# Fixing TensorE's instruction order in a decode-attention plus MLP kernel: mask products, PV rounds and output products at new places

## The chip, the cores and the metric

The kernel runs on one core of one Trainium2 chip. The metric is the device time of one execution in microseconds (us). The time before is the median of 8 executions. Engines are named as the profile names them: PE is TensorE (PEld its weight loads), DVE is VectorE, ACT is ScalarE, POOL is GpSimd, SP is SyncE, whose queue issues nearly all of the DMAs.

## The reference

Two blocks share one input of two rows and are added to it. Block A is one decode step of attention over the last 2048 positions of a cache, and block B is a squared-ReLU MLP.

```python
B, Sq, D = 2, 1, 576;  Hq, Hkv, Sk, Dh = 32, 16, 8192, 128;  F = 4608
W = min(4096, max(256, Sk // 4))                       # 2048
xn = (x - mean(x)) / sqrt(var(x) + 1e-5)
# A: attention of one query position, two query heads to a KV head
q = (xn @ wq).reshape(B, Sq, Hq, Dh).transpose(0, 2, 1, 3)
k = repeat(k_cache[:, :, Sk - W:, :], 2, axis=1);  v = repeat(v_cache[:, :, Sk - W:, :], 2, axis=1)
p = softmax(einsum("bhqd,bhkd->bhqk", q, k) * Dh ** -0.5)
attn = einsum("bhqk,bhkd->bhqd", p, v).transpose(0, 2, 1, 3).reshape(B, Sq, Hq * Dh) @ wo
# B: MLP
h = relu(einsum("bsd,df->bsf", xn, w1) + b1) ** 2
return x + attn + einsum("bsf,fd->bsd", h, w2) + b2
```

All tensors are bf16. Together 53.6 MB are read from HBM: 16.8 MB of K, as much of V, and the four weights.

## The kernel before, in words

**Units.** Attention is cut into 8 units, each of 4 KV heads of one batch row (`u` in the code; `NU` is 8). A unit's K is one DMA of 2 MB, its V another. Both go into a pool of six buffers (`kvpool`), which later also takes three of the five pieces of `w2`. A load waits until the unit that had its buffer has read it for the last time: K in its transposes, V in its PV products.

**One step.** `step(u)` does these things for a unit:

- `transposes(u, g)`, g from 0 to 7: four products with an identity (line 288) turn K tiles of f32 pairs into the PSUM tile `kT_ps`, of which there are three. Even groups are copied out by ACT (line 293), odd ones by DVE (line 295).
- `scores(u, 0)` after group 5 and `scores(u, 1)` after group 7: eight products each (line 307) into `sc_ps`, of which there are two. The first product of a unit is the head mask product (line 301): it writes a large negative number wherever a query row and a key belong to different heads.
- `softmax(u)`: a row maximum on DVE (`mx`, line 316), a maximum over partitions on POOL (`gmax`), the bias `nb` on DVE, the exponential on ACT (`pr`, line 327) and a transpose on DVE (`pT`, line 329).
- For unit u-2: `pv_sum` (line 339: the sums of the softmax, put together by one small f32 product), four rounds of `pv` (line 352: four products each), the mixing of the four PV parts by four chained DVE operations into `acc` (lines 361 and 364), and `pv_out` (line 376: the "o product", one small f32 product that puts `acc` into the layout for `wo`).

**Ends.** Units 0 to 3 and 4 to 7 are gathered in two halves. After a half is complete, DVE forms `ws` (lines 381, 385), and `wo_acc` multiplies it with half of `wo` (32 products, line 239) into `out_ps`. The MLP's first product (`mlp_h_block`, line 406), its squared ReLU and nine transposes (line 420) stand between unit 6 and unit 7. Its second product (`mlp_o`, line 239) comes after everything of the attention, and its last piece (`mlp_tail`, line 442) closes the kernel. It is followed by one addition on DVE and two small stores.

**Order.** A scheduler orders the instructions of each engine by what is ready; the DMAs on SP stay in the order in which they are traced. An instruction given to `tc.keep_in_program_order` keeps the traced order among those so marked on its engine. In the kernel before, only the products of `scores` and `pv` and the four that put x and b2 into `out_ps` are marked. So the scheduler placed the rest of PE's work: the head mask product of a unit stands one step ahead, in front of the transposes of the step before its own, and at the end of a step the o product of unit u-2 and the sum product of unit u-1 stand in front of that mask product. The order of PE at a step's end before is therefore: four PV rounds, `scores(u, 1)`, o product of u-2, sum product of u-1, mask product of u+2, transposes of u+1.

Of the kernel before, what the change touches and what calls it, by code (L numbers as in the profile page):

```python
# [16 lines left out]
def kernel(  # L17
# [68 lines left out]
    keep = ctx.enter_context(tc.tile_pool(name="keep", bufs=3))  # L86
    psum = ctx.enter_context(tc.tile_pool(name="psum", bufs=1, space=bass.MemoryType.PSUM))

    x2d = A_x.rearrange("b s d -> (b s) d")
# [110 lines left out]
    for c in range(NFULL):  # L200
        nc.tensor.transpose(out=pro_ps[:, c, :], in_=xn_sb[:, c:NFULL * P:NFULL], identity=ident[:B, :B])  # L201
    for sg in range(S):
        nc.tensor.transpose(out=pro_ps[:, NFULL + sg, :], in_=xr_sb[:, sg, :], identity=ident[:B, :B])
    xnT = const.tile([P, NXN, B], BF16, name="xnT")
# [31 lines left out]

    def out_acc(lhsT, rhs_of, start=False, stop=False, pin=False):
        for i in range(2):
            mm = nc.tensor.matmul(out_ps[32 * i:32 * i + B, :], lhsT=lhsT, rhs=rhs_of(i * OH, (i + 1) * OH),  # L239
                                  start=start, stop=stop, skip_group_check=True)  # L240
            if pin:
                tc.keep_in_program_order(mm)

# [6 lines left out]
    def q_block(c):  # L250
        for k in range(2):
            for g in range(NG4):
                rhs, xc = w_rows(wq_tiles, c, g * QW + k * QB, QB, LQ)
                nc.tensor.matmul(q_ps[k][32 * g:32 * g + B, :], lhsT=xnT[:, xc, :], rhs=rhs,  # L254
                                 start=(c == 0), stop=(c == KC - 1), skip_group_check=True,
                                 tile_position=(0, 32 * g))
        if c == KC - 1:
            qrow = const.tile([RB, QW], BF16, tag="row", name="qrow")
            nc.vector.tensor_copy(out=qrow[:, 0:QB], in_=q_ps[0][0:RB, :])
            nc.scalar.copy(out=qrow[:, QB:QW], in_=q_ps[1][0:RB, :])  # L260
            qT_ps = psum.tile([P, QH, P], BF16, tag="misc", name="qT_ps")
            for i in range(QH):
                nc.tensor.transpose(out=qT_ps[:, i, 0:RB], in_=qrow[:, i * Dh:(i + 1) * Dh],
                                    identity=ident[0:RB, 0:RB])
            qT_v = qT_ps[:].rearrange("p i (g s) -> p i g s", s=32)
            for b in range(B):
                nc.vector.tensor_copy(out=qT_all[:, b, :].rearrange("p (g i) -> p i g", g=NG4), in_=qT_v[:, :, :, b])
            qe_ps = psum.tile([P, 2 * NU, NC], F32, tag="sm", name="qe_ps")
            for e in range(2):
                nc.tensor.matmul(qe_ps[:, e * NU:(e + 1) * NU, :], lhsT=par[:, e, :, :].rearrange("p a i -> p (a i)"),  # L270
                                 rhs=qT_all[:].rearrange("p b h -> p (b h)"), start=True, stop=True)
# [7 lines left out]
    def transposes(u, g):  # L279
# [6 lines left out]
        for i in range(PG):  # L286
            q = g * PG + i
            nc.tensor.transpose(out=kT_ps[:, i, :], in_=k_sb[:, 2 * q * Dh:2 * (q + 1) * Dh].bitcast(F32),  # L288
                                identity=ident_f[:])
# [7 lines left out]
    def scores(u, w):  # L297
        tq, b = divmod(u, B)
        if w == 0:
            sc_tiles[u] = psum.tile([P, NT, 32], F32, tag="sc", bufs=2, name=f"sc_ps_{u}")  # L300
            nc.tensor.matmul(sc_tiles[u][:].rearrange("p t s -> p (t s)"), lhsT=qhead[:], rhs=khead[:],  # L301
                             start=True, stop=False, skip_group_check=True)
        sc_ps = sc_tiles[u]
        kT = kT_tiles.pop((u, w))[:].rearrange("p t s e -> p e t s")
        for e in range(2):
            for k in range(4):
                mm = nc.tensor.matmul(sc_ps[32 * k:32 * (k + 1), :, :],  # L307
                                      lhsT=qz[:, e, b * NQ + tq, w, :, :].rearrange("p j c -> p (j c)"),
                                      rhs=kT[:, e, :, 32 * k:32 * (k + 1)], start=False, stop=(w == 1 and e == 1),
                                      skip_group_check=True, tile_position=(0, 32 * k))  # L310
                tc.keep_in_program_order(mm)

# [21 lines left out]
    def pv_sum(u):  # L334
        tq, b = divmod(u, B)
        if u % (2 * B) == 0:
            sm_tiles[tq // 2] = psum.tile([P, B * Dh + 2 * B], F32, tag="sm", name=f"sm_{tq // 2}")
        rs = sm_tiles[tq // 2][:, B * Dh + u % (2 * B):B * Dh + u % (2 * B) + 1]
        nc.tensor.matmul(rs, lhsT=samec[:].rearrange("p x c -> p (x c)"), rhs=sum_tiles.pop(u)[:],
                         start=True, stop=True, skip_group_check=True)  # L340
# [6 lines left out]
    def pv(u, i):  # L347
        pv_ps, f = pv_cur[u]
        v = v_tiles[u][:].rearrange("p (w t x) -> p t w x", w=2, t=NT)
        for k in range(4):  # L350
            t = 4 * i + k
            mm = nc.tensor.matmul(pv_ps[32 * k:32 * (k + 1), :, :].rearrange("m (w a) d -> m w (a d)", w=2),  # L352
                                  lhsT=pT_tiles[u][:, t, :], rhs=v[:, t, :, :], start=(i == 0),
                                  stop=(i == NT // 4 - 1), skip_group_check=True, tile_position=(0, 32 * k))
            tc.keep_in_program_order(mm)
        if i == NT // 4 - 1:
            acc = None
            for j in range(4):
                nx = work.tile([P, Dh], F32, tag=f"acc{j % 2}", name=f"acc_{u}_{j}")
                if j == 0:  # L360
                    nc.vector.tensor_scalar(out=nx[:], in0=pv_ps[:, j, :], scalar1=f[:, j:j + 1], scalar2=None,  # L361
                                            op0=ALU.mult)
                else:
                    nc.vector.scalar_tensor_tensor(out=nx[:], in0=pv_ps[:, j, :], scalar=f[:, j:j + 1], in1=acc[:],  # L364
                                                   op0=ALU.mult, op1=ALU.add)
                acc = nx
            pv_cur[u] = acc
            pT_tiles.pop(u)

    wo_state = {}  # L370

    def pv_out(u):
        tq, b = divmod(u, B)
        t, half = divmod(tq, 2)
        sm = sm_tiles[t]
        nc.tensor.matmul(sm[half * (P // 2):(half + 1) * (P // 2), b * Dh:(b + 1) * Dh],  # L376
                         lhsT=tohead[:].rearrange("p c x -> p (c x)"), rhs=pv_cur.pop(u)[:], start=True, stop=True,
# [18 lines left out]
    def mlp_h_start():  # L396
        mlp["ps"] = [psum.tile([P, HB], F32, tag="kT", bufs=3, name=f"h_ps_{k}") for k in range(3)]
        for k in range(3):
            nc.tensor.matmul(mlp["ps"][k][:], lhsT=sel4[:], rhs=b1_sb[:, k * HB:(k + 1) * HB],
                             start=True, stop=False, skip_group_check=True)  # L400

    def mlp_h_block(c):
        for k in range(3):
            for g in range(NG4):
                rhs, xc = w_rows(w1_tiles, c, g * HW + k * HB, HB, L1)
                nc.tensor.matmul(mlp["ps"][k][32 * g:32 * g + B, :], lhsT=xnT[:, xc, :], rhs=rhs,  # L406
                                 start=False, stop=(c == KC - 1), skip_group_check=True,
                                 tile_position=(0, 32 * g))

    def mlp_h_end():  # L410
# [8 lines left out]
        for r in range(FR):  # L419
            nc.tensor.transpose(out=ha[:, r, 0:RB], in_=hrow[:, r:HW:FR], identity=ident[0:RB, 0:RB])  # L420
        for g in range(NG4):
# [12 lines left out]
    def mlp_tail(r0, r1):  # L434
# [4 lines left out]
        for r in range(r0, r1):  # L439
            o = (r - r0) * D  # L440
            for i in range(4):
                nc.tensor.matmul(mlp["out"][32 * i:32 * i + B, :], lhsT=mlp["h"][:, (NG4 - 1) * FR + r, :],
                                 rhs=w2_sb[:, o + i * OQ:o + (i + 1) * OQ], start=(r == 0), stop=(r == FR - 1),
# [16 lines left out]
    load_k(3)  # L460

    def pv_all(u):
        pv_sum(u)
        for i in range(NT // 4):
            pv(u, i)
        pv_out(u)

    def step(u, with_pv=True):
        with_pv = with_pv and u >= 2
        if with_pv:  # L470
            pv_sum(u - 2)
# [28 lines left out]
    load_k(4)  # L500
    out_acc(ident[:B, :B], lambda a, z: x_sb[:, a:z], start=True, pin=True)
    out_acc(ones_b[:, :], lambda a, z: b2_sb[:, a:z], pin=True)
    for u in range(2, NU - 1):
# [24 lines left out]
    for w in W2P[:NG4 - 1]:  # L528
# [42 lines left out]
```

## Time and profile before

| | us |
|---|---|
| median of 8 executions | 136.63 |
| their range | 134.99 to 138.31 |
| the profiled execution, its own time | 135.37 |
| its span, first to last instruction | 133.2 |
| PE busy, weight loads busy | 90.6 (68%), 58.0 (44%) |
| DVE busy, ACT busy | 62.2 (47%), 46.9 (35%) |
| share of the 16 DMA engines in the main queue | 94.7% of the span |

The profiled execution is one execution of its own; 2.2 us of its time lie outside the span. Matmuls are pipelined on PE, so that its busy time is not time at its peak. "Idle before" in the rows is time in which the engine stood still before the named instruction, and the arrow names what ended it. The row PEclk of the page gives the clock that the throttle granted to TensorE, in tenths.

### The profile page before, as it was taken

Reading aid. Unit: us, or ns where it says so; the run is one execution under the profiler, and the core shown is the slowest. Engines: PE = TensorE matmul, PEld = TensorE weight load, DVE = VectorE, ACT = ScalarE, POOL = GpSimd, SP = SyncE. Lnnn points to the kernel's source line nnn. Section 1 sums busy time; section 2 is a strip of 40 time slices with the busy share of each in tenths; the row PEclk is TensorE's granted clock in tenths of the full one; section 3 lists DMA queues with packets and bytes.
Section 4 is the critical chain, followed back from the end, with each engine's and each line's share of the span. In section 5 each row is a group of like instructions: output and inputs, shape, how many; then the busy total and the mean of one; then the engine's idle time right before and its main releaser. Section 6 shows DMA issues by size and latency. Waiting matters only on the chain.

```text
span 133.2 us, 2061 instructions
## 1 busy us (share of the span) xinstructions
PE 90.6 (68%) x838; PEld 58.0 (44%) x838; DVE 62.2 (47%) x169; ACT 46.9 (35%) x63; POOL 7.5 (6%) x21
## 2 busy tenths in 40 slices
PE   0059658798369759929956948996498497056980
PEld 0059212285047349418615718842353463023650
DVE  6914403265543664573486477357500565643010
ACT  5707401187255326623715715632001283200010
POOL 7500000010100010010010010001000000100000
PEclk9999985569986995995999995599558999965897
DMA  3999999999999999999999999999999999999940
GB/s 114 415 415 443 423 423 433 428 433 418 445 413 448 418 433 428 438 423 433 433 428 428 428 432 432 423 437 437 420 428 438 418 438 439 410 417 436 413 178 1
DMA packets 4268, 53.74 MB, mean 404 GB/s; under 512 B 542, under 2 KB 544, under 8 KB 1060
## 3 DMA queue, kind: packets, MB, share of 16 engines
q1 hardware_dynamic: 4184, 53.61, 94.7%
q8 instruction: 6, 0.10, 0.3%
q0 software_dynamic: 64, 0.01, 0.0%
q14 instruction: 2, 0.02, 0.0%
q10 hardware_dynamic: 12, 0.00, 0.0%
HBM read 53.62 MB, written 0.00 MB: 403 GB/s over the span
## 4 chain that ended last, share of the span: by engine, by line
PE 39%; DMA 33%; DVE 13%; ACT 5%; issue 3%; SPq 2%; POOL 2%; ACTq 0%; POOLq 0%; DVEq 0%
PE kT_ps L288 22%; DMA w<-in_B_w_dram 20%; DMA wq<-in_A_wq_dram 12%; PE sc_ps L307 5%; PE pv_ps L352 4%; DVE acc L364 3%; ACT pr L327 3%; PE out_ps L239 3%; DVE mx L316 3%; ACT kT L293 2%; PE sc_ps L301 2%; POOL gmax L320 2%; DVE acc L361 2%; DVE kT L295 2%; PE q_ps L254 1%
## 5 line engine op out<-in xcount | busy, mean ns | idle before, releaser
L288 PE MATMUL kT_ps<-ident_f,k 128*128 128x128 f32 x256 | 43.0, 332 | 3.1 <-DMA k<-in_A_k_cache_dram 1.5
L288 PEld LDWEIGHTS kT_ps<-ident_f,k 128*128 128x128 f32 x256 | 37.1, 174 | 15.9 <-issue 7.6
L293 ACT COPY kT<-kT_ps 128x1024 bf16<-128x1024 bf16 x32 | 32.0, 1012 | 26.7 <-PE kT_ps L288 26.5
L295 DVE COPY kT<-kT_ps 128x1024 bf16<-128x1024 bf16 x32 | 22.1, 691 | 28.1 <-PE kT_ps L288 28.0
L376 PE MATMUL sm<-acc,tohead 128*64 128x128 f32 x16 | 3.9, 333 | 14.7 <-DVE acc L364 14.7
L327 ACT ACTIVATE pr<-sc_ps,nb 128x512 bf16<-128x512 f32 x8 | 5.5, 687 | 21.8 <-DVE nb L324 18.3
L307 PE MATMUL sc_ps<-kT,qz 128*32 128x512 bf16 x128 | 10.9, 425 | 2.6 <-DVE kT L295 1.6
L376 PEld LDWEIGHTS sm<-acc,tohead 128*64 128x64 f32 x16 | 1.7, 152 | 18.9 <-DVE acc L364 16.7
L320 POOL PARTITION_ALL_REDUCE gmax<-m x8 | 2.9, 364 | 104.6 <-DVE m L318 104.6
L352 PE MATMUL pv_ps<-v,pT 128*32 128x512 bf16 x128 | 8.7, 392 | 0.0
L364 DVE SCALAR_TENSOR_TENSOR acc<-pv_ps,f,acc 128x128 f32<-128x128 f32 x24 | 8.3, 346 | 0.5
L239 PE MATMUL out_ps<-wo,ws 128*2 128x288 bf16 x64 | 7.4, 417 | 1.1 <-DVE ws L385 1.1
L316 DVE TENSOR_REDUCE mx<-sc_ps 128x1 f32<-128x512 f32 x8 | 5.5, 684 | 3.8 <-PE sc_ps L307 3.8
L301 PE MATMUL sc_ps<-khead,qhead 4*128 4x512 bf16 x8 | 3.7, 459 | 4.8 <-ACT pr L327 4.8
L329 DVE STREAM_TRANSPOSE pT<-pr 128x512 bf16<-128x512 bf16 x8 | 5.7, 710 | 2.4 <-ACT pr L327 2.3
L239 PEld LDWEIGHTS <-ws 128*2 128x2 bf16 x64 | 3.6, 116 | 4.4 <-DVE ws L385 1.5
L532 ACT COPY part<-out_ps 2x144 f32<-2x144 f32 x2 | 0.5, 268 | 14.0 <-DVE part L532 14.0
L307 PEld LDWEIGHTS <-qz 128*32 128x32 bf16 x128 | 2.2, 99 | 6.8 <-DVE kT L295 3.5
L415 ACT ACTIVATE t<-h_ps 98x384 f32<-98x384 f32 x3 | 1.4, 488 | 10.1 <-PE h_ps L406 9.8
L201 PE MATMUL pro_ps<-ident,xn_sb 2*128 2x2 bf16 x4 | 0.3, 173 | 6.7 <-DVE xn_sb L192 6.7
L416 DVE TENSOR_TENSOR hrow<-t 98x384 bf16<-98x384 f32 x3 | 1.6, 555 | 6.6 <-ACT t L415 6.5
L254 PE MATMUL q_ps<-wq,xnT 128*2 128x512 bf16 x32 | 2.5, 447 | 2.9 <-DMA wq<-in_A_wq_dram 2.9
(88 smaller groups left out, 66.3 us busy)
## 6 DMA issues: line engine op xcount, KB each, us to landing
k<-in_A_k_cache_dram SPq DMA_DIRECT2D x8, 2048.0 KB, 21.2
v<-in_A_v_cache_dram SPq DMA_DIRECT2D x8, 2048.0 KB, 25.4
wo<-in_A_wo_dram SPq DMA_DIRECT2D x2, 2304.0 KB, 17.4
w<-in_B_w_dram SPq DMA_DIRECT2D x2, 2304.0 KB, 24.7
wq<-in_A_wq_dram SPq DMA_DIRECT2D x2, 2048.0 KB, 14.0
w<-in_B_w_dram SPq DMA_DIRECT2D x3, 1296.0 KB, 22.3
w<-in_B_w_dram SPq DMA_DIRECT2D x1, 1008.0 KB, 26.9
w_rem<-in_B_w_dram SPq DMA_DIRECT2D x1, 576.0 KB, 28.1
```

The source lines that it names most:

```text
L239: mm = nc.tensor.matmul(out_ps[32 * i:32 * i + B, :], lhsT=lhsT, rhs=rhs_of(i * OH, (i + 1) * OH), start=start, stop=stop, skip_group_chec ...
L288: nc.tensor.transpose(out=kT_ps[:, i, :], in_=k_sb[:, 2 * q * Dh:2 * (q + 1) * Dh].bitcast(F32), identity=ident_f[:])
L293: nc.scalar.copy(out=dst, in_=src)
L295: nc.vector.tensor_copy(out=dst, in_=src)
L301: nc.tensor.matmul(sc_tiles[u][:].rearrange("p t s -> p (t s)"), lhsT=qhead[:], rhs=khead[:], start=True, stop=False, skip_group_check=True)
L307: mm = nc.tensor.matmul(sc_ps[32 * k:32 * (k + 1), :, :], lhsT=qz[:, e, b * NQ + tq, w, :, :].rearrange("p j c -> p (j c)"), rhs=kT[:, e, ...
L316: nc.vector.tensor_reduce(out=mx[:], in_=sc_ps, axis=AX.X, op=ALU.max)
L327: nc.scalar.activation(out=pr[:], in_=sc_ps, func=ACT.Exp, bias=nb[:], scale=scale, accum_out=sums[:])
L329: nc.vector.transpose(out=pT[:].rearrange("p t m -> p (t m)"), in_=pr[:])
L352: mm = nc.tensor.matmul(pv_ps[32 * k:32 * (k + 1), :, :].rearrange("m (w a) d -> m w (a d)", w=2), lhsT=pT_tiles[u][:, t, :], rhs=v[:, t, ...
L364: nc.vector.scalar_tensor_tensor(out=nx[:], in0=pv_ps[:, j, :], scalar=f[:, j:j + 1], in1=acc[:], op0=ALU.mult, op1=ALU.add)
L376: nc.tensor.matmul(sm[half * (P // 2):(half + 1) * (P // 2), b * Dh:(b + 1) * Dh], lhsT=tohead[:].rearrange("p c x -> p (c x)"), rhs=pv_cu ...
```

## The change

Every PE instruction goes through `pe_mm` or `pe_tr`, which mark it to keep its traced order; the four DVE operations that mix the PV parts are marked too. With the order fixed, the traced places decide, and four of these are changed:

- The head mask product stands where it is traced, in front of `scores(u, 0)` of its own unit, after transposes of group 5.
- In a step, `pv_sum(u - 2)` comes after the transposes of group 1, and the four PV rounds stand after groups 1, 2, 3 and 4. Before, all four stood after group 7.
- The mixing of the PV parts (`pv_mix`) is a function of its own, traced after group 7.
- The o product `pv_out(u - 2)` goes into the next step, after the transposes of group 1.

Between unit 6 and unit 7, `wo_acc(0)` follows right after the PV products of unit 5; unit 5's o product comes after the MLP's nine transposes. `pv_sum(6)` comes behind `scores(7, 1)`. In the built kernel, PE's order at a step's end is: `scores(u, 1)`, transposes of groups 0 and 1 of u+1, o product of u-2, sum product of u-1, then PV rounds and transposes in turn. The DMAs on SP keep their order. The orders of DVE and ACT stay the same within the steps but for one exchange: `od` and `ws` of the first half and the scale of a unit (`ri`, `f`) now come behind the DVE copy of group 1.

```diff
+    def pe_mm(out, **kw):
+        return tc.keep_in_program_order(nc.tensor.matmul(out, **kw))
+
+    def pe_tr(**kw):
+        return tc.keep_in_program_order(nc.tensor.transpose(**kw))
...
     def pv(u, i):
         pv_ps, f = pv_cur[u]
         v = v_tiles[u][:].rearrange("p (w t x) -> p t w x", w=2, t=NT)
         for k in range(4):
             t = 4 * i + k
-            mm = nc.tensor.matmul(pv_ps[32 * k:32 * (k + 1), :, :].rearrange("m (w a) d -> m w (a d)", w=2),
+            pe_mm(pv_ps[32 * k:32 * (k + 1), :, :].rearrange("m (w a) d -> m w (a d)", w=2),
                                   lhsT=pT_tiles[u][:, t, :], rhs=v[:, t, :, :], start=(i == 0),
                                   stop=(i == NT // 4 - 1), skip_group_check=True, tile_position=(0, 32 * k))
-            tc.keep_in_program_order(mm)
-        if i == NT // 4 - 1:
-            acc = None
...
+    def pv_mix(u):
+        pv_ps, f = pv_cur[u]
+        acc = None
...
+            tc.keep_in_program_order(op)
+            acc = nx
+        pv_cur[u] = acc
+        pT_tiles.pop(u)
...
+    NR = NT // 4
+
     def pv_all(u):
         pv_sum(u)
-        for i in range(NT // 4):
+        for i in range(NR):
             pv(u, i)
-        pv_out(u)
+        pv_mix(u)
 
     def step(u, with_pv=True):
         with_pv = with_pv and u >= 2
-        if with_pv:
-            pv_sum(u - 2)
         for g in range(NG):
             transposes(u, g)
+            if with_pv and g == 1:
+                if u >= 3:
+                    pv_out(u - 3)
+                pv_sum(u - 2)
+            if with_pv and 1 <= g <= NR:
+                pv(u - 2, g - 1)
             if g == GW + 1:
                 scores(u, 0)
         if with_pv:
-            for i in range(NT // 4):
-                pv(u - 2, i)
+            pv_mix(u - 2)
         scores(u, 1)
-        if with_pv:
-            pv_out(u - 2)
         softmax(u)
...
     mlp_h_start()
+    pv_out(NU - 4)
     pv_all(NU - 3)
     wo_acc(0)
     for c in range(KC):
         mlp_h_block(c)
     mlp_h_end()
+    pv_out(NU - 3)
     step(NU - 1, with_pv=False)
     pv_all(NU - 2)
+    pv_out(NU - 2)
     pv_all(NU - 1)
+    pv_out(NU - 1)
     wo_acc(1)
```

More of the change, by code (lines that the diff above doesn't have):

```diff
@@ L200 @@
     for c in range(NFULL):
-        nc.tensor.transpose(out=pro_ps[:, c, :], in_=xn_sb[:, c:NFULL * P:NFULL], identity=ident[:B, :B])
+        pe_tr(out=pro_ps[:, c, :], in_=xn_sb[:, c:NFULL * P:NFULL], identity=ident[:B, :B])
     for sg in range(S):
-        nc.tensor.transpose(out=pro_ps[:, NFULL + sg, :], in_=xr_sb[:, sg, :], identity=ident[:B, :B])
+        pe_tr(out=pro_ps[:, NFULL + sg, :], in_=xr_sb[:, sg, :], identity=ident[:B, :B])
     xnT = const.tile([P, NXN, B], BF16, name="xnT")
@@ L235, with out_acc @@
     nc.vector.memset(out_ps[:], 0.0)
-    def out_acc(lhsT, rhs_of, start=False, stop=False, pin=False):
+    def out_acc(lhsT, rhs_of, start=False, stop=False):
         for i in range(2):
-            mm = nc.tensor.matmul(out_ps[32 * i:32 * i + B, :], lhsT=lhsT, rhs=rhs_of(i * OH, (i + 1) * OH),
-                                  start=start, stop=stop, skip_group_check=True)
-            if pin:
-                tc.keep_in_program_order(mm)
+            pe_mm(out_ps[32 * i:32 * i + B, :], lhsT=lhsT, rhs=rhs_of(i * OH, (i + 1) * OH),
+                  start=start, stop=stop, skip_group_check=True)
     qT_all = const.tile([P, B, Hq], BF16, name="qT_all")
@@ L253, in q_block @@
                 rhs, xc = w_rows(wq_tiles, c, g * QW + k * QB, QB, LQ)
-                nc.tensor.matmul(q_ps[k][32 * g:32 * g + B, :], lhsT=xnT[:, xc, :], rhs=rhs,
+                pe_mm(q_ps[k][32 * g:32 * g + B, :], lhsT=xnT[:, xc, :], rhs=rhs,
                                  start=(c == 0), stop=(c == KC - 1), skip_group_check=True,
@@ L262, in q_block @@
             for i in range(QH):
-                nc.tensor.transpose(out=qT_ps[:, i, 0:RB], in_=qrow[:, i * Dh:(i + 1) * Dh],
+                pe_tr(out=qT_ps[:, i, 0:RB], in_=qrow[:, i * Dh:(i + 1) * Dh],
                                     identity=ident[0:RB, 0:RB])
@@ L269, in q_block @@
             for e in range(2):
-                nc.tensor.matmul(qe_ps[:, e * NU:(e + 1) * NU, :], lhsT=par[:, e, :, :].rearrange("p a i -> p (a i)"),
+                pe_mm(qe_ps[:, e * NU:(e + 1) * NU, :], lhsT=par[:, e, :, :].rearrange("p a i -> p (a i)"),
                                  rhs=qT_all[:].rearrange("p b h -> p (b h)"), start=True, stop=True)
@@ L287, in transposes @@
             q = g * PG + i
-            nc.tensor.transpose(out=kT_ps[:, i, :], in_=k_sb[:, 2 * q * Dh:2 * (q + 1) * Dh].bitcast(F32),
+            pe_tr(out=kT_ps[:, i, :], in_=k_sb[:, 2 * q * Dh:2 * (q + 1) * Dh].bitcast(F32),
                                 identity=ident_f[:])
@@ L300, in scores @@
             sc_tiles[u] = psum.tile([P, NT, 32], F32, tag="sc", bufs=2, name=f"sc_ps_{u}")
-            nc.tensor.matmul(sc_tiles[u][:].rearrange("p t s -> p (t s)"), lhsT=qhead[:], rhs=khead[:],
+            pe_mm(sc_tiles[u][:].rearrange("p t s -> p (t s)"), lhsT=qhead[:], rhs=khead[:],
                              start=True, stop=False, skip_group_check=True)
@@ L306, in scores @@
             for k in range(4):
-                mm = nc.tensor.matmul(sc_ps[32 * k:32 * (k + 1), :, :],
+                pe_mm(sc_ps[32 * k:32 * (k + 1), :, :],
                                       lhsT=qz[:, e, b * NQ + tq, w, :, :].rearrange("p j c -> p (j c)"),
@@ L310, in scores @@
                                       skip_group_check=True, tile_position=(0, 32 * k))
-                tc.keep_in_program_order(mm)
     def softmax(u):
@@ L338, in pv_sum @@
         rs = sm_tiles[tq // 2][:, B * Dh + u % (2 * B):B * Dh + u % (2 * B) + 1]
-        nc.tensor.matmul(rs, lhsT=samec[:].rearrange("p x c -> p (x c)"), rhs=sum_tiles.pop(u)[:],
+        pe_mm(rs, lhsT=samec[:].rearrange("p x c -> p (x c)"), rhs=sum_tiles.pop(u)[:],
                          start=True, stop=True, skip_group_check=True)
@@ L351, in pv @@
             t = 4 * i + k
-            mm = nc.tensor.matmul(pv_ps[32 * k:32 * (k + 1), :, :].rearrange("m (w a) d -> m w (a d)", w=2),
+            pe_mm(pv_ps[32 * k:32 * (k + 1), :, :].rearrange("m (w a) d -> m w (a d)", w=2),
                                   lhsT=pT_tiles[u][:, t, :], rhs=v[:, t, :, :], start=(i == 0),
                                   stop=(i == NT // 4 - 1), skip_group_check=True, tile_position=(0, 32 * k))
-            tc.keep_in_program_order(mm)
-        if i == NT // 4 - 1:
-            acc = None
[L358 to L368, printed above, removed]
+    def pv_mix(u):
+        pv_ps, f = pv_cur[u]
+        acc = None
+        for j in range(4):
+            nx = work.tile([P, Dh], F32, tag=f"acc{j % 2}", name=f"acc_{u}_{j}")
+            if j == 0:
+                op = nc.vector.tensor_scalar(out=nx[:], in0=pv_ps[:, j, :], scalar1=f[:, j:j + 1], scalar2=None,
+                                             op0=ALU.mult)
+            else:
+                op = nc.vector.scalar_tensor_tensor(out=nx[:], in0=pv_ps[:, j, :], scalar=f[:, j:j + 1], in1=acc[:],
+                                                    op0=ALU.mult, op1=ALU.add)
+            tc.keep_in_program_order(op)
+            acc = nx
+        pv_cur[u] = acc
+        pT_tiles.pop(u)
     wo_state = {}
@@ L375, in pv_out @@
         sm = sm_tiles[t]
-        nc.tensor.matmul(sm[half * (P // 2):(half + 1) * (P // 2), b * Dh:(b + 1) * Dh],
+        pe_mm(sm[half * (P // 2):(half + 1) * (P // 2), b * Dh:(b + 1) * Dh],
                          lhsT=tohead[:].rearrange("p c x -> p (c x)"), rhs=pv_cur.pop(u)[:], start=True, stop=True,
@@ L398, in mlp_h_start @@
         for k in range(3):
-            nc.tensor.matmul(mlp["ps"][k][:], lhsT=sel4[:], rhs=b1_sb[:, k * HB:(k + 1) * HB],
+            pe_mm(mlp["ps"][k][:], lhsT=sel4[:], rhs=b1_sb[:, k * HB:(k + 1) * HB],
                              start=True, stop=False, skip_group_check=True)
@@ L405, in mlp_h_block @@
                 rhs, xc = w_rows(w1_tiles, c, g * HW + k * HB, HB, L1)
-                nc.tensor.matmul(mlp["ps"][k][32 * g:32 * g + B, :], lhsT=xnT[:, xc, :], rhs=rhs,
+                pe_mm(mlp["ps"][k][32 * g:32 * g + B, :], lhsT=xnT[:, xc, :], rhs=rhs,
                                  start=False, stop=(c == KC - 1), skip_group_check=True,
@@ L419, in mlp_h_end @@
         for r in range(FR):
-            nc.tensor.transpose(out=ha[:, r, 0:RB], in_=hrow[:, r:HW:FR], identity=ident[0:RB, 0:RB])
+            pe_tr(out=ha[:, r, 0:RB], in_=hrow[:, r:HW:FR], identity=ident[0:RB, 0:RB])
         for g in range(NG4):
@@ L441, in mlp_tail @@
             for i in range(4):
-                nc.tensor.matmul(mlp["out"][32 * i:32 * i + B, :], lhsT=mlp["h"][:, (NG4 - 1) * FR + r, :],
+                pe_mm(mlp["out"][32 * i:32 * i + B, :], lhsT=mlp["h"][:, (NG4 - 1) * FR + r, :],
                                  rhs=w2_sb[:, o + i * OQ:o + (i + 1) * OQ], start=(r == 0), stop=(r == FR - 1),
@@ L500 @@
     load_k(4)
-    out_acc(ident[:B, :B], lambda a, z: x_sb[:, a:z], start=True, pin=True)
-    out_acc(ones_b[:, :], lambda a, z: b2_sb[:, a:z], pin=True)
+    out_acc(ident[:B, :B], lambda a, z: x_sb[:, a:z], start=True)
+    out_acc(ones_b[:, :], lambda a, z: b2_sb[:, a:z])
     for u in range(2, NU - 1):
```

## Prediction, made before the changed kernel was run

> **What bounds the kernel now.** I read the page's 40 slices first, to see which resource never rests.
>
> ```profile
> PEclk9999985569986995995999995599558999965897
> DMA  3999999999999999999999999999999999999940
> GB/s 114 415 415 443 423 423 433 428 433 418 445 413 448 418 433 428 438 423 433 433 428 428 428 432 432 423 437 437 420 428 438 418 438 439 410 417 436 413 178 1
> ```
>
> DMA is at 9 in every slice from the second to the third from the end, at some 430 GB/s. PE shows 68% of the span. So the transfers look like the bound, and the question is whether the queue could ever run dry, and what PE does when the last piece lands. SP's timeline answers the first.
>
> ```profile
> 66.51 0.54 SPq L105 DMA_DIRECT2D v<-in_A_v_cache_dram  x1
> ...
> 100.10 0.34 SPq L136 DMA_DIRECT2D wo<-in_A_wo_dram  x1
> 100.49 2.33 SPq L149 DMA_DIRECT2D w<-in_B_w_dram  x5
> ```
>
> A load is issued when PE frees its buffer, but it lands much later: the page gives 21.2 us (K) and 25.4 us (V) from issue to landing as medians, for 2.1 MB that take 4.9 us at 430 GB/s. The rest is queue in front of it. The thinnest place is the issue at 66.51: what was issued before it still needs until about 74 (count back from `w_rem`, which is issued at 68.67 and lands 28.1 us later, at 96.8: its own 0.6 MB take 1.4 us, w1's 4.7 MB 11.0, wo's 2.4 MB 5.5 and this V 4.9). Some 7 us of queue stay, so PE starves no transfer.
>
> The end of PE's timeline answers the second.
>
> ```profile
> 116.41 0.43 PE L376 MATMUL sm<-acc,tohead 128*64 128x128 f32 x2 [3.37 <-DVE acc L364]
> ...
> 121.87 3.40 PE L239 MATMUL out_ps<-wo,ws 128*2 128x288 bf16 x32 [1.13 <-DVE ws L385]
> 125.10 3.47 PE L239 MATMUL out_ps<-w,hT_sb 128*2 128x288 bf16 x54
> 128.87 1.01 PE L442 MATMUL tail_ps<-w,hT_sb 128*2 128x144 bf16 x36 [0.29 <-DMA w<-in_B_w_dram]
> ```
>
> PE ends its queue of work at 128.57 and waits 0.29 us for the last big piece of `w2`; the chain of waits ends on the very last piece (issued at 102.38, landed 27.16 later, at 129.54). **Two chains end within 0.3 us of each other**: the stream of transfers, and PE's chain from step to step. The second one is not steady from execution to execution, as a table of four steps (each from one row maximum to the next) shows.
>
> ```profile
> 45.97:56.97 11.00, 8.50 (x69) 6.29 (x69) 6.15 (x17) 4.83 (x6) 0.37 (x1) 0.84 1.01 429
> 56.97:68.24 11.27, 8.61 (x69) 5.91 (x69) 6.15 (x16) 4.76 (x6) 0.36 (x1) 0.85 1.02 436
> 68.24:78.11 9.87, 7.13 (x69) 4.59 (x69) 6.15 (x17) 4.73 (x6) 0.36 (x1) 1.00 1.01 432
> 78.11:89.94 11.83, 9.95 (x71) 7.27 (x71) 6.95 (x19) 4.83 (x6) 0.36 (x1) 0.71 0.99 424
> ```
>
> The columns are length, then busy time of PE, PEld, DVE, ACT, POOL, then granted clock, DMA share and GB/s. With nearly the same work a step takes 9.87 us at clock 1.00 and 11.83 at 0.71. The step at 9.87 keeps pace with its two loads (2 x 4.9 us); the others fall behind the data. Likewise the 32 products at 121.87 ran at half clock with 106 ns each, the 54 behind them at full clock with 64 ns each: one such stretch alone is worth 32 x 42 ns = 1.35 us. Where in the kernel the slow stretches fall is likely to differ between executions, and with 0.29 us of slack nearly all of it is paid. The profiled execution took 135.37 us, near the lowest (134.99), and the median is 1.26 above it. I read the lower end as the stream's floor, and the rest as a late PE chain.
>
> **The change, part by part.** The idle places of PE that it touches:
>
> ```profile
> PE sm L376 <- DVE acc L364: 14.7, 8, 3.4
> ...
> PE sc_ps L301 <- ACT pr L327: 4.8, 4, 2.5
> ```
>
> *Mask product at its scores.* At 21.43 and 22.40 two of them stand between the q transposes, 0.53 and 0.54 us on the chain of waits. Unit 0's now runs while PE waits 1.02 us for the qz copies anyway, unit 1's inside step 1 (0.38 us, where unit 2's was at 30.92). Gain at the start: 1.1 us. At the step ends the 4.8 us of waiting for `pr` go.
>
> *O product into the next step.* After the scores of step 3 end at 56.61, PE stood idle 1.66 us for `acc`, ran the two small products, stood idle 0.80 us for `pr`, ran a mask product and began transposes at 60.33, 3.7 us after. Now groups 0 and 1 fill that gap, and group 2 uses the third `kT_ps`. What is late next is ACT: its copy of group 0 is queued behind `pr`, which ends at 59.76, so the copy ends at 60.8 and group 3 can't start before 4.2 us after the scores. The o product still waits for `acc`; behind it on PE stand the PV rounds and group 2, and they have until 4.2 us, so its wait costs nothing.
>
> *PV between transposes.* From group 3 on stand 5 groups (12 transposes take 1.57 us at full clock, so 0.52 a group), two PV rounds (a quarter of 1.05 each), mask product and first scores (0.95), DVE's copy of group 7 (0.69, no longer covered by PV) and the second scores (0.6): 5.4 us. A step is then 4.2 + 5.4 = 9.6 us at full clock, against 9.87 measured; at half clock (20 transposes in 3.71, 0.74 a group) about 11.3 against 11.83. I take 0.5 us a step over five steps, 2.5 us, with ends at 0 and 1.5 a step[...].
>
> Here a rule speaks against the change. The Trainium skill, "TensorE: Matmul & The Clock Gate" (Part 3, what overlaps and what doesn't), says that a weight load overlaps running products only when its row group differs. Transposes and PV rounds both use all 128 rows, and splitting PV in four adds six switches a step: by the rule three loads of a K tile (174 ns mean) and three of `pT` (34 ns), 0.6 us a step, which eats the gain. The trace has this switch: the last transposes before PV run from 54.82 to 55.20 and PV begins at 55.13, with no idle before its row. By the row it is 0. I take the row; the 0.6 goes into the range.
>
> *Between units 6 and 7.* Before, `wo_acc(0)` started at 96.06, 6.5 us after the scores of step 6 (89.58), behind the o product of unit 5, which waits 1.96 us for `acc`, and the sum product of unit 6. Now only these stand before it: the bias products, the wait of 1.66 for `acc` of unit 4, 0.8 for two small products, and PV in 1.05: 3.4 us. That is 3.1 us earlier.
>
> The sum: step 6 ends at 89.6 - 1.1 - 2.5 = 86.0, `wo_acc(0)` runs from 89.4 to 92.9, and then the MLP waits for data: `w_rem` at 96.8, the product ends near 97.4 (before 102.84), its transposes near 100.1. K of unit 7 lands at 96.8 + 4.9 = 101.7, so step 7 starts there and not at 105.87. From its start to `wo_acc(1)` took 16.0 us; the mask product inside, the sum product behind the scores and the two small DVE operations ahead of `m` add 1.2: 118.9, with `wo` (100.10 + 17.4 = 117.5) there. 3.4 and two thirds of 3.47 follow: 124.6. The third piece of `w2` lands at about 126.5 (1.0 MB ahead of 128.86), PE is done at 127.7, and waits about 1.2 us for the piece at 128.86. PE could be 3.1 us later and lose nothing.
>
> So in the profiled execution the end does not move: the last piece lands at 129.54 as before, **135.37 - 0 = 135.4 us**. It is the median that moves, down to that floor. Between the profiled 135.37 and the lowest 134.99 I forecast 135.2 us, 1.0% under the median. SP's order and the transfers are untouched, so I see nothing that ends below 134.3.
>
> **The rivals.**
>
> 1. *The spread is the stream's own.* Stretches of 10 us run at 421 to 437 GB/s; 1% over 126 us is 1.3 us. Then the floor moves from execution to execution, PE's new slack is worth at most the few tenths by which it was late, and the time is 136.3. Against it: the four steps, whose length follows the clock. Chance 0.22.
>
> 2. *Slower: the fixed order blocks PE at `kT_ps`.* While group 3 waits for ACT's copy of group 0, the scheduler's freedom to put something else there is gone, and the rounds and scores behind it wait too; with switches at the rule's price and copies that fall out of step, a step gets longer. Place: groups 3 to 7. Point: step 6 then needs to end 5.8 us later than without any gain in the steps (1.4 us to `w_rem`, 1.3 to K of unit 7, 3.1 at the end), so 1.2 us a step over today's 11.0. At 13 us a step the loads fall behind as well: 5 x 2 - 5.8 = 4.2 us, 139.6. Against it: ACT's busy time a step is 4.8 of 11 us. Chance 0.12.
>
> 3. *The order is fixed, but the stalls stay*, as waits for copies in place of waits for `acc`, and the MLP is no earlier: 136.6. Chance 0.06.
>
> **How the numbers follow.** The forecast has 0.60, with its own range of 134.4 to 136.0. About 1% is what a measurement of this kernel can tell from no change; the line lies at 135.26, so the forecast is split, 0.37 faster and 0.23 within. Rival 1 gives 0.02 faster and 0.19 within, rival 3 is mostly within, rival 2 is slower. With a little for what I don't see: faster 0.40, within 1% 0.44, slower 0.16. The range, 134.3 to 137.3, takes in the forecast, rivals 1 and 3, and leaves rival 2 out.
>
> **What would show it.** Right: L376 and L301 nearly without idle time; transposes starting within 0.2 us of a step's second scores; `wo_acc(0)` before 92; step 7 starting on the landing of its K, near 102; a wait for `w2` over 1 us before the last products; last landing again near 129.5. Wrong: steps over 12 us with idle time on `kT_ps`, a last product that waits for PE alone, or a DMA share under 9 in the middle. If PE has its slack and the executions still spread over 3 us, rival 1 holds.

## Result, and the profile after

| | before | after |
|---|---|---|
| median | 136.33 us (53 executions) | 134.74 us (18 executions) |
| range | 134.98 to 138.80 | 134.60 to 135.03 |
| profiled execution, own time | 135.37 | 134.69 |
| its span | 133.2 | 132.9 |

The 8 executions given for the kernel before are among these 53. The change makes the kernel 1.6 us faster by the medians (134.74 / 136.33 = 0.988). The measured ratio is **0.991, 95% interval 0.9885 to 0.9935**; it leaves out executions more than 1.5% above a kernel's fastest, and such executions are part of what the change removes, so the gain in it is the smaller of the two.

The lowest times differ by only 0.38 us, and this part lies outside the span from the first to the last instruction. On average 2.17 us lie outside before (2.10 to 2.24 in 63 executions of it that were made beside the runs below) and 1.81 after (1.75 to 1.86); the lowest spans are 132.7 and 132.8 us. So within the span the floor is the same, and what is gone there is the upper part of the spread.

First the slices of the page after, as shown for before, and then the two lines of its section on the chain that ended last (shares by engine, then by line).

```profile
PEclk9999999599658999999999975698698599955999
DMA  3999999999999999999999999999999999999940
GB/s 129 406 431 429 429 434 414 449 409 444 422 434 434 424 434 424 439 424 439 414 444 419 449 435 424 427 416 433 420 452 414 434 433 439 403 434 429 415 193 1
...
DMA 87%; PE 7%; SPq 3%; issue 0%; DVE 0%; DVEq 0%
DMA k<-in_A_k_cache_dram 66%; DMA w<-in_B_w_dram 21%; PE kT_ps L93 5%; SPq L111 1%; PE pv_ps L90 1%; SPq L118 1%; PE sc_ps L90 1%; SPq L123 0%; PE tail_ps L90 0%; DVE fin_sb L550 0%; PE sm L90 0%; DVEq L550 0%
```

The stream is what it was. The chain has changed hands: it was 39% PE and 33% DMA, now it is 87% DMA. PE's timeline at the end shows why (start, length, then operation, and in brackets the idle time and what ended it):

```profile
101.88 4.50 PE L93 MATMUL kT_ps<-ident_f,k 128*128 128x128 f32 x24
...
118.70 4.00 PE L90 MATMUL out_ps<-wo,ws 128*2 128x288 bf16 x32 [1.13 <-DVE ws L390]
122.50 2.51 PE L90 MATMUL out_ps<-w,hT_sb 128*2 128x288 bf16 x36
126.31 1.27 PE L90 MATMUL out_ps<-w,hT_sb 128*2 128x288 bf16 x18 [1.30 <-DMA w<-in_B_w_dram]
128.73 0.97 PE L90 MATMUL tail_ps<-w,hT_sb 128*2 128x144 bf16 x36 [1.16 <-DMA w<-in_B_w_dram]
```

Step 7 starts at 101.88 (before 105.87; its K landed at 101.74), and PE now waits twice for `w2`, 1.30 and 1.16 us, where it waited 0.29 once. The last piece lands at 129.36 (before 129.54). The wait for `acc` in front of the o products is down from 14.7 to 6.8 us; the one of the mask product for `pr` is gone.

```profile
PE sm L90 <- DVE acc L368: 6.8, 7, 2.6
```

### The profile page after: what moved, and what is told of

Its sections match the earlier page's. It is cut to its first block, busy times and chain, and to the rows that moved or that the text cites. A ratio compares the mean times of both kernels' runs of the same rounds, so it can differ in the third digit from the quotient of the medians.

```text
span 132.9 us, 2060 instructions
## 1 busy us (share of the span) xinstructions
PE 91.5 (69%) x838; PEld 56.2 (42%) x838; DVE 61.3 (46%) x169; ACT 46.4 (35%) x63; POOL 7.5 (6%) x21
## 4 chain that ended last, share of the span: by engine, by line
DMA 87%; PE 7%; SPq 3%; issue 0%; DVE 0%; DVEq 0%
DMA k<-in_A_k_cache_dram 66%; DMA w<-in_B_w_dram 21%; PE kT_ps L93 5%; SPq L111 1%; PE pv_ps L90 1%; SPq L118 1%; PE sc_ps L90 1%; SPq L123 0%; PE tail_ps L90 0%; DVE fin_sb L550 0%; PE sm L90 0%; DVEq L550 0%
## 5 line engine op out<-in xcount | busy, mean ns | idle before, releaser
L93 PE MATMUL kT_ps<-ident_f,k 128*128 128x128 f32 x256 | 44.7, 327 | 5.9 <-DMA k<-in_A_k_cache_dram 4.2
L93 PEld LDWEIGHTS kT_ps<-ident_f,k 128*128 128x128 f32 x256 | 35.0, 168 | 17.9 <-issue 7.6
L90 PE MATMUL sc_ps<-kT,qz 128*32 128x512 bf16 x128 | 9.8, 385 | 6.3 <-DVE kT L299 5.5
L90 PE MATMUL pv_ps<-v,pT 128*32 128x512 bf16 x128 | 12.8, 441 | 0.0
L90 PE MATMUL sm<-sums,samec 128*128 128x1 f32 x16 | 3.3, 276 | 3.1 <-DVE od L386 3.1
L90 PEld LDWEIGHTS <-pT 128*32 128x32 bf16 x128 | 3.2, 97 | 4.2 <-issue 3.5
L90 PEld LDWEIGHTS <-hT_sb 128*2 128x2 bf16 x90 | 3.0, 85 | 4.3 <-issue 1.7
L90 PEld LDWEIGHTS sm<-sums,samec 128*128 128x128 f32 x16 | 2.8, 221 | 4.6 <-DVE od L386 3.4
```

The lines of the kernel that those rows point to most:

```text
L90: return tc.keep_in_program_order(nc.tensor.matmul(out, **kw))
L93: return tc.keep_in_program_order(nc.tensor.transpose(**kw))
```

## The experiments

Two theories of where the gain comes from. **Theory 1**: two chains end together, the stream of loads with a floor near 134.7 and PE's chain, whose length follows the clock; the change puts slack between them. In form **1a** the slack comes from the work between units 6 and 7, in **1b** from the shorter steps. **The rival**: the stream sets the end in both kernels, and it is the stream's own spread that was seen. Neither form names two more parts of the change, the mask products at their scores and the fixed order itself; they come up with u_all.

### A load taken out: PE's chain by itself

One V load less moves the stream's floor by 4.9 us, so that PE's chain shows in the time. The edit to both kernels, and what two of the runs undo in the changed one:

```diff
         if u == 5:
-            load_v(NU - 1)
+            v_tiles[NU - 1] = v_tiles[NU - 2]
```

> The kernel before, without the load of V of unit 7 (2.1 MB, the unit takes V of unit 6 instead). Theory 1, the end is set by PE's chain in most executions: the stream ends 4.9 us earlier and this gains only what PE waited, so about 135.9 with a spread of 3 us as before. Rival, the stream sets the end in both kernels and the spread is its own: 136.3 - 4.9 = 131.4.

> The changed kernel, without the load of V of unit 7 (unit 7 takes V of unit 6). Theory 1: the stream's floor goes to 134.7 - 4.9 = 129.8, and PE's chain, freed of its waits of 1.30 and 1.16 us for w2, sets the end: about 132.3, now with the spread of a PE chain (1 to 3 us), and 3.5 to 4 us under the kernel before with the same load left out. Rival, PE's chain was not shortened and the stream was what changed: no difference between the two kernels without this load beyond the 1.6 us of the full ones.

```diff
# su_mlp, beside it
     pv_all(NU - 3)
+    pv_out(NU - 3)
+    pv_sum(NU - 2)
     wo_acc(0)
...
     mlp_h_end()
-    pv_out(NU - 3)
     step(NU - 1, with_pv=False)
-    pv_all(NU - 2)
+    for i in range(NR):
+        pv(NU - 2, i)
+    pv_mix(NU - 2)
```

> As s_after, V of unit 7 left out, with one part undone: the first half of the wo products again behind the o product of unit 5 and the sum product of unit 6, as in the kernel before. Theory 1a, the place of these products between unit 6 and unit 7 carries the gain: the MLP ends 3 us later, past the landing of K of unit 7, so 2.5 to 3 us over s_after. Theory 1b, the steps carry it: within 0.5 us of s_after.

```diff
# su_steps, beside it; head_mask(u) is the mask product, made at scores(u, 0) if not before
...
-            if with_pv and g == 1:
-                if u >= 3:
-                    pv_out(u - 3)
-                pv_sum(u - 2)
-            if with_pv and 1 <= g <= NR:
-                pv(u - 2, g - 1)
...
         if with_pv:
+            for i in range(NR):
+                pv(u - 2, i)
             pv_mix(u - 2)
         scores(u, 1)
+        if with_pv:
+            pv_out(u - 2)
+        if 1 <= u < NU - 2:
+            pv_sum(u - 1)
+        if 2 <= u < NU - 2 and u + 2 < NU - 1:
+            head_mask(u + 2)
...
     mlp_h_start()
-    pv_out(NU - 4)
```

> As s_after, V of unit 7 left out, with the three moves inside the steps undone (four PV rounds after group 7, o product and sum product at the end of the step, mask product ahead of the next transposes), the order between units 6 and 7 as changed. Theory 1a: the chain waits for w_rem and K of unit 7 anyway, within 0.7 us of s_after. Theory 1b: steps longer by 0.5 to 1 us each put step 6 and all behind it later, 2 to 3 us over s_after.

| V of unit 7 not loaded | median us (range) | against s_after |
|---|---|---|
| s_before | 136.07 (133.26 to 138.92) | +2.88 |
| s_after | 133.19 (131.82 to 133.51) | |
| su_mlp | 135.83 (134.46 to 136.22) | +2.64 |
| su_steps | 133.78 (132.70 to 134.49) | +0.59 |

s_after and su_steps are 4 executions each, the other two 10. The kernel before loses 4.9 us of loads and gets 0.3 us faster at the median. Its highest time stays (138.92), its lowest falls by 1.6 us (133.26 for 134.90 with all loads on the same chip). So in its fastest executions the stream had set the end, and in most of them it does not: the rival falls. With the load out of the way, the changed kernel is 2.88 us ahead by the medians, less than the 3.5 to 4 expected, and 1.44 by the lowest.

Putting back the wo products costs 2.64 us, putting back the steps 0.59. How the loads decide this is seen at step 7, in s_after, then in su_mlp, then in su_steps:

```profile
101.96 3.74 PE L93 MATMUL kT_ps<-ident_f,k 128*128 128x128 f32 x20 [1.13 <-DMA k<-in_A_k_cache_dram]
...
113.68 0.43 PE L90 MATMUL sm<-acc,tohead 128*64 128x128 f32 x2 [2.59 <-DVE acc L368]
```

```profile
104.35 1.49 PE L93 MATMUL kT_ps<-ident_f,k 128*128 128x128 f32 x12
...
115.94 0.43 PE L90 MATMUL sm<-acc,tohead 128*64 128x128 f32 x2 [4.15 <-DVE acc L368]
```

```profile
95.37 1.81 PE L90 MATMUL h_ps<-w,xnT 128*2 128x384 bf16 x24 [4.31 <-DMA w<-in_B_w_dram]
...
101.90 4.77 PE L93 MATMUL kT_ps<-ident_f,k 128*128 128x128 f32 x24 [0.47 <-DMA k<-in_A_k_cache_dram]
```

In s_after PE is early and waits 1.13 us for K of unit 7. In su_steps step 6 reaches its second scores at 81.78, six us before s_after (87.75), and nothing of it is left at step 7: PE waits 4.31 us for `w` and 0.47 for K, and starts it at 101.90. **What PE saved ahead of these landings was worth nothing.** Of the 0.59 us, 0.36 lie outside the span (2.17 us outside, against 1.80 in s_after); the median spans differ by 0.25.

In su_mlp step 7 starts 2.4 us late, but the 2.64 us are not the place of the wo products alone. The edit also puts the mixing of unit 6 behind `pT` of unit 7 on DVE, so that from the second scores of step 7 to the o product of unit 6 it takes 5.63 us (110.31 to 115.94), against 4.50 in s_after and 4.85 in the kernel before. The lowest su_mlp (134.46) is slower than the lowest s_before (133.26). With these 1.1 us taken off, an estimate for the place is 1.5 us. **1a is the largest single part found, 1.5 to 2.6 of 2.88 us**; what the rest is made of, these runs do not separate.

### Places undone with all loads kept

u_mlp is su_mlp's order with all loads kept. u_all adds the order of su_steps to it. The fixed order stays, and so do the mask products of units 0 to 3 and 7 at their scores: only those of units 4 to 6 go back. With unit 3's the longest wait for `pr` is gone too (2.45 us of the 4.8 before).

> The changed kernel, all loads kept, with only the first half of the wo products put back behind the o product of unit 5 and the sum product of unit 6. Theory 1a: PE's chain loses 2.6 us of its slack (su_mlp against s_after) and is back at the edge, median 135.2 to 136.2, lowest 134.6, spread 1 to 2 us. Theory 1b: 134.7 within 0.4.

> The changed kernel with every place undone, only the fixed order kept: PV rounds after group 7, small products and mask product at the end of the step, wo products of the first half behind the o product of unit 5. Theory: fixing the order is worth nothing by itself, 136.0 to 136.5 with a spread of 3 us. If the fixed order alone made the difference: 134.7 within 0.4.

u_mlp: median 134.94 us (134.49 to 138.16). Six of ten executions lie below 135, at the floor, and three between 137.7 and 138.2. By the median this is what 1b expected, and not 1a's 135.2 to 136.2; by the spread the long tail is back. So with all loads in place the other parts alone mostly give enough slack, and in three of ten executions they do not. How much of that is the place of the wo products is not shown: like u_all, this run has the wait for `acc` in it (4.14 us) that neither kernel has.

u_all: 135.85 us (134.99 to 136.64), beside 136.82 (134.88 to 138.94) for the kernel before on the same chip. I had expected nothing from it, and at the median it gained 1.0 us, with the same lowest time. At a mean clock of 0.797 it takes 136.6 us, where the kernel before takes 138.3 to 138.9 at 0.796. Its products from `qT_all` start at 21.67 as in the changed kernel, and not at 23.00, since the two mask products between the q transposes are gone. Whether these, the mask product of unit 3 or the fixed order carry the gain is open: a run with the fixed order and all mask products at their old places was not made.

### Work added near the end: the slack itself

```diff
+    zero_b = const.tile([P, B], BF16, name="zero_b")
+    nc.gpsimd.memset(zero_b[:], 0.0)
...
+    wo_sb1 = wo_tiles[1]
     wo_acc(1)
+    for r in range(16):                      # 32 in d_after64p
+        out_acc(zero_b[:, :], lambda a, z: wo_sb1[:, r % WR, a:z])
```

> The kernel before with 32 more products of a zero weight with the same wo tile behind the last wo products (64 ns each at full clock, 106 at half: 2.0 to 3.4 us on PE near the end; they add zeros). Theory 1, PE's chain sets the end in most executions: 136.3 + 2.0 to 3.4 less the 0.3 us of slack, 138.0 to 139.4. Rival, the stream sets it: 136.3.

> The changed kernel with the same 32 zero products. Theory 1: they go into the waits of 1.30 and 1.16 us for w2 and the slack behind them, 134.7 to 135.2. If the slack that was predicted (3.1 us) is not there: 136 to 138.

> The changed kernel with 64 zero products, 4.1 to 6.8 us. Theory 1: the slack is used up, so 1 to 3.5 us over the changed kernel, 135.8 to 138.2, and the spread of a PE chain comes back. If PE had far more slack than 3 us: 134.7.

d_before32p: 139.22 us (138.62 to 140.04), 2.6 over the kernel before, as theory 1 has it. d_after64p: 138.25 (136.51 to 139.18), at the upper edge of what was expected. But d_after32p took 136.09 (135.82 to 136.90), a miss. In its profiled execution, the fastest of the ten, PE no longer waits for `w2`, but the end is still a landing, at 130.42 in place of 129.36. The stream ran at 426 GB/s between 20 and 120 us, and so it did in the other two kernels with the tile `zero_b`. Two more runs took the tile and the work apart:

```diff
# z_after32p: same work, no new tile
...
+        out_acc(qz[:, 0, 0, 0, 2, 0:B], lambda a, z: wo_sb1[:, r % WR, a:z])
...
# z_pad: the tile alone, never read
+    zero_b = const.tile([P, B], BF16, name="zero_b")
+    nc.gpsimd.memset(zero_b[:], 0.0)
```

> The changed kernel with 32 zero products again, their weight now taken from zeros that the qz tile holds anyway, so that no tile is added (they add zeros). If what cost 1.4 us in d_after32p was PE's work: 136.1 again, last landing near 130.4. If it was the stream, slowed by the tile that was added (it ran at 425 GB/s from 20 to 120 us where the changed kernel ran at 430): 134.7 to 135.2, last landing near 129.4.

> The changed kernel with nothing but the small tile of zeros of d_after32p added and never used (4 bytes a partition, in front of the pools of the loads). Tile slows the stream: 135.5 to 136.0, at 425 GB/s. It doesn't: 134.7.

z_pad: 135.67 us (135.66 to 135.80): **the tile by itself costs 0.9 us**, on a kernel whose executions otherwise lie within 0.43 us (u_mlp, on the same chip and without the tile, reached 134.49). The rows for 20 to 120 us (length, busy time of PE, PEld, DVE, ACT, POOL, then clock, DMA share, GB/s), of the changed kernel and of z_pad:

```profile
20.00:120.00 100.00, 74.97 (x654) 44.90 (x652) 51.62 (x133) 37.28 (x51) 2.92 (x8) 0.86 1.01 429
```

```profile
20.00:120.00 100.00, 73.92 (x644) 43.77 (x642) 51.73 (x133) 37.19 (x51) 2.93 (x8) 0.86 1.01 426
```

The engines are as busy for as long, and the stream is 0.7% slower at the same DMA share. The tile stands in the pool ahead of those into which the loads write; that it shifts their addresses, and that this is the cause, is a guess which no run here tested.

z_after32p: 135.90 us (134.93 to 136.49), near the 136.1 that was expected if PE's work was the cost, and without the tile. So the tile alone costs 0.9 us, the work alone 1.2, and both together 1.35. Here the stream ran at 429 GB/s, and PE was late in the profiled execution (136.49, the slowest of the ten):

```profile
102.02 5.35 PE L93 MATMUL kT_ps<-ident_f,k 128*128 128x128 f32 x24 [0.97 <-DMA k<-in_A_k_cache_dram]
...
115.97 1.90 PE L90 MATMUL pv_ps<-v,pT 128*32 128x512 bf16 x16
...
121.30 3.99 PE L90 MATMUL out_ps<-wo,ws 128*2 128x288 bf16 x32 [1.13 <-DVE ws L390]
125.09 2.16 PE L90 MATMUL out_ps<-wo,qz 128*2 128x288 bf16 x32
```

Step 7 again starts on the landing of its K, at 102.02, but its first 24 transposes take 5.35 us (4.50 after) and PV of unit 7 1.90 us (1.05 at full clock). The wo products then start 19.3 us after the step, against 16.8 in the profile after. The 32 zero products add 2.0 us to that, until the next products start at 127.08. So the slack is no fixed number: it depends on where the slow stretches fall, and the 2.46 us of the profile after were not there in most executions.

### One wait more taken away

> The changed kernel with one move more: in the step of unit 6 the o product of unit 3 stands after transposes of group 0, so that DVE forms od ahead of its copy of group 1 and the sum product of unit 4 doesn't wait 3.11 us for it. Theory 1: step 6 and the wo products end 2 to 3 us earlier, but w_rem (96.9) and K of unit 7 (101.7) hold PE up all the same, so 134.7 as the changed kernel. If the steps carry the end: lower by up to 1 us.

```diff
-            if with_pv and g == 1:
+            if with_pv and g == (0 if u == 2 * B + 2 else 1):
                 if u >= 3:
                     pv_out(u - 3)
-                pv_sum(u - 2)
+            if with_pv and g == 1:
+                pv_sum(u - 2)
```

134.67 us (134.56 to 134.74), not told apart from the changed kernel's 134.74. But the edit did not do what was expected of it. The wait got shorter and did not go:

```profile
76.58 0.43 PE L90 MATMUL sm<-acc,tohead 128*64 128x128 f32 x2 [0.86 <-DVE acc L368]
...
79.52 0.59 PE L90 MATMUL sm<-sums,samec 128*128 128x1 f32 x2 [1.92 <-DVE od L386]
```

The sum product starts 0.48 us earlier (79.52 for 80.00), and the second scores of step 6 are where they were (88.90 for 88.95), not 2 to 3 us earlier. The wo products start at 92.52 in place of 93.05, because PV of unit 5 ran in 1.05 us and not in 1.58. So this run can't tell what the wait costs; that earlier work of PE ends in the next landing rests on su_steps.

## Why the prediction was right, point by point

- **Two chains, and a floor.** Forecast 135.2 us; measured 134.74. The profiled execution was to stay at 135.4 and took 134.69, with a last landing at 129.36 for a forecast "near 129.5". Of these 0.68 us, 0.38 lie outside the span, which the prediction did not look at, 0.18 are the landing and 0.12 what follows it.
- **The spread was PE's.** Rival 1 of the prediction fell: the spread went from 3.8 to 0.43 us.
- **The path to it was in part luck.** PE was to be 6.7 us earlier at the first wo products (96.06 to 89.4) and was 3.0 earlier, from the order between units 6 and 7 alone: the start and the steps had given nothing by the end of step 6. That this cost no time is due to the landings behind it, to which the forecast left 3.9 us (92.9 to 96.8). In the profile after PE doesn't wait there at all: it comes to step 7 at 101.88, with K landed at 101.74.
- **The start**: 1.1 us forecast; `qe` starts 1.33 us earlier (21.67 for 23.00). But then PE waits for K of unit 2, and with a slow stretch behind that wait, the second scores of step 2 start at 45.37, later than before (45.01):

```profile
35.47 1.97 PE L93 MATMUL kT_ps<-ident_f,k 128*128 128x128 f32 x8 [2.57 <-DMA k<-in_A_k_cache_dram]
```

- **Steps**: 9.6 us at full clock forecast, 9.66 to 9.68 measured in three steps, in the windows from one second half of the scores to the next (columns as above). The first part, up to group 3, took 3.97 us (4.2 forecast), the second 5.71 (5.4). At half clock 11.3 was forecast from 0.74 us a group, which was read from a stretch at a clock of 0.63; at 0.51 a group took 1.05 us (81.06 to 82.11 after, with its switch to PV). The last window is step 6:

```profile
45.37:55.05 9.68, 7.98 (x71) 4.62 (x71) 5.93 (x16) 4.62 (x6) 0.37 (x1) 1.00 1.00 427
...
64.71:74.39 9.68, 8.01 (x69) 4.62 (x70) 5.94 (x16) 4.62 (x6) 0.37 (x1) 1.00 1.00 426
74.39:88.95 14.56, 10.24 (x69) 5.73 (x70) 6.94 (x18) 4.72 (x6) 0.37 (x1) 0.77 1.01 431
```

- **Where row and rule differed, I chose wrongly.** I priced the switches between transposes and PV at 0 by one row, against an estimate of 0.6 us a step by the rule of the Trainium skill, "TensorE: Matmul & The Clock Gate" (Part 3, what overlaps and what doesn't). After, from the start of group 3 to the mask product stand 3 groups and 2 PV rounds:

```profile
49.88 0.66 PE L93 MATMUL kT_ps<-ident_f,k 128*128 128x128 f32 x4 [0.40 <-ACT kT L297]
50.47 0.40 PE L90 MATMUL pv_ps<-v,pT 128*32 128x512 bf16 x4
50.80 0.66 PE L93 MATMUL kT_ps<-ident_f,k 128*128 128x128 f32 x4
51.38 0.40 PE L90 MATMUL pv_ps<-v,pT 128*32 128x512 bf16 x4
51.71 0.66 PE L93 MATMUL kT_ps<-ident_f,k 128*128 128x128 f32 x4
52.30 0.39 PE L90 MATMUL sc_ps<-khead,qhead 4*128 4x512 bf16 x1
```

They take 2.42 us from start to start. Without switches they would take 3 x 0.50 (12 transposes from 107.63 to the scores at 109.13 before) and 2 x 0.22 (16 PV products from 55.13 to the scores at 56.00 before), 1.94. The four switches cost 0.48 us, 0.12 each. The estimate has 0.10 each, from 174 ns for a load of K and 34 for one of `pT`; the second is a sixteenth of a row in which loads overlap, and with their own mean of 95 ns it would be 0.13. The price fits the rule; that PE waits for the loads in these places is not shown. The step came out right all the same, since the part up to group 3 was taken too long. The 0.40 of idle time on the first row is the wait for ACT's copy that was forecast.
- **The wait that I missed.** Step 6 was to end at 86.0 and the wo products to start at 89.4; they were 89.6 (the same as before) and 93.05, after the 92 that was given as a sign. The last window above is that step, 14.56 us; before, it took 11.83 (77.15 to 88.98), and what the steps ahead of it had gained (74.39 for 77.15) was lost in it. PE's timeline names the term:

```profile
76.45 0.43 PE L90 MATMUL sm<-acc,tohead 128*64 128x128 f32 x2 [0.42 <-DVE acc L368]
80.00 0.58 PE L90 MATMUL sm<-sums,samec 128*128 128x1 f32 x2 [3.11 <-DVE od L386]
```

`sm` has one PSUM buffer. Unit 4's sum product opens its second use, and so waits until DVE has read the first half in `od`. On DVE, `od` now stands behind the copy of group 1, and that behind `pT`, which waits for `pr` (0.57 us of wait before, 3.11 now). After it the clock is 0.51 up to 85.29; whether the wait brought this is not tested. The order given ahead of the prediction showed the wait; I had counted what stood behind the o product and not what stood ahead of `od`. What it cost in the time no run isolates.
- **Between units 6 and 7**: step 7 on the landing of its K, near 102: 101.88. The first wo products start 3.48 us after the end of step 6 (3.4 forecast). The wo products of the second half: 118.9 forecast, 118.70. The last wait: 1.2 forecast, 1.16.
- **The slack of 3.1 us** was mis-sized. The profile after has 1.30 + 1.16 = 2.46. The second wo products took 3.80 us where 3.4 were allowed, at a clock of 0.50, and the third piece of `w2` came at 126.31 for 126.5. From the start of step 7 to these products I allowed 17.2 us; the profiles of the kernels with this order have 16.8 to 19.3, by where the slow stretches fall. I had used the spread of the clock to explain the median, and then left it out of the slack.

## What to carry to other kernels

When two chains end together, the profiled execution shows one of them, and the spread of many executions shows the other: here the lowest span stayed while the median fell, and that was slack, not less work. Look for the next landing behind each saving; what PE saved ahead of a load that it had to wait for was worth nothing, and the largest single part came from an order change by which PE stopped missing such a landing. Count the slack with its own variation, and at a buffer with a single copy follow the reader's queue too. An experiment that puts one part back can bring in a wait that neither kernel had; compare its waits with those of both before reading its time as the price of that part.

## What the runs showed of the hardware that was not expected

- **Time and clock.** For 63 executions of the kernel before, time and mean granted TensorE clock are both on record. The 17 below 135.5 us have a mean clock of 0.854, the 22 from there to 137 0.822, the 8 up to 138 0.807, the 16 above 0.796 (correlation -0.95). The changed kernel's 18 span 0.842 to 0.896 and stay within 0.43 us (correlation -0.13): its time no longer follows the clock. Its clock is also higher, so that slack and clock may both have had a part in the smaller spread; no run separates them.
- **Time outside the span.** With the steps in the order of before (before, s_before, d_before32p, su_steps, u_all) 2.15 to 2.18 us lie outside the first to the last instruction on average, with the steps as changed 1.78 to 1.89. This is about 0.36 of the 1.59 us between the two kernels' medians. What happens in this time no profile here shows.
- **Four bytes a partition.** An unused small tile ahead of the pools that loads write to cost 0.9 us of 135, as a stream slower by 0.7% from 20 to 120 us. Other sizes and places were not tested; an edit made for an experiment can bring in such a cost by accident.
